# Loading q and k by tile pairs, values in quadrants, and shorter first blocks in a chunked attention and gated FFN kernel

## The chip, the core and the metric

The kernel runs on one core of a Trainium2 chip. The metric is device time in microseconds (us), as a median of several executions. A profile of one execution shows what each engine did: TensorE (PE, and PEld for its weight loads), VectorE (DVE), ScalarE (ACT), GpSimd (POOL, which here only issues DMAs and fills buffers) and SyncE (SP, which issues others).

## The reference

Four batches, eight heads, 768 positions, head dimension 64. Attention works on chunks of 32 queries: each sees 8 memory keys, 16 positions to the left of the chunk, the chunk and 8 to its right. The result, 3072 tokens of 512 features, goes through a gated feed-forward network (FFN) of 1536 hidden features.

```python
for c in range(nc):                       # 24 chunks of 32
    k_full = concat([mem_k, k[l_start:r_end]]); v_full = concat([mem_v, v[l_start:r_end]])
    scores = scale * (q_c @ k_full.T)
    a = softmax(scores)
    out[c] = a @ v_full
x = out.transpose(0, 2, 1, 3).reshape(3072, 512)
y = (relu(x @ w_gate) * (x @ w_val)) @ w_out
```

## The kernel before, in words

Work goes by tiles of 128 tokens (four chunks): 24 tiles, six to a batch, each with all eight heads. Head pairs share the 128 partitions.

For each tile, `load_qk` (L185) has POOL issue one DMA each for q and k, 1024 reads of 64 f32 (256 bytes), converted to bf16. `qk_t` (L206) transposes them on PE, four 128x128 transposes per operand, and `qk_copy` (L212) brings the result from PSUM to `qT` or `kT` on ACT or DVE. `scores` (L224) runs 32 small matmuls in tiles of 64 rows by 32 columns. Then come `row_max` (with memsets for the two edges of a batch, L245 and L247), `subtract`, three `exponent` runs on ACT, `row_sum`, `reciprocal` and `normalise`. `p_t` (L281) transposes the probabilities, `p_copy` copies them. `values` (L291) runs 16 matmuls, one for each chunk and head pair: its weights are a 128x128 block-diagonal of two heads' values in `v_bd` (56 context rows and 8 memory rows for each head, zeros off the diagonal). `x_copy` (L301) writes x transposed into `xT`.

`v_bd` has two sets of buffers. The first gets its zeros and memory rows from DVE (`pattern_spread`, L157), the second its zeros from POOL (`zero`, L114), its memory rows by 8 DMAs on SP for each batch (`mem_rows`, L138). Value rows come by POOL's DMAs (`load_v_rows`, L164), for the first batch in two halves of three tiles.

The FFN goes by blocks of tiles, `BLOCKS = [3, 3, 4, 4, 4, 4, 2]`. `first` (L311) computes for a block and a hidden group m (12 of 128 features) the gate and the value product, four matmuls each (one tile's part of the four is called a tile-group in the prediction). `relu` on ACT and `gate` on DVE follow, and `second` (L333) multiplies by `w_out`, 12 matmuls for a tile. `w_gate` and `w_val` arrive in four groups of three m each, four DMAs to a group; blocks 0 and 1 are interleaved by these groups.

The order on each engine is written out by a planner, `schedule` (L518), before launch. Each operation has its engines, an estimated cost, what it must follow, buffers that it takes and gives, and a priority; the planner simulates the engines and always starts the ready operation of lowest priority number. Attention stands before FFN, and later tiles are held to the pace of the FFN block before theirs (`pace`, L390). Loads go to POOL strictly in the order in which they are listed (L475 to L513): q and k of the first tiles, the first half of the values, the rest of q and k, the first group of weights, the second half of the values, the other weights with the zero fills, memory values, `w_out` between q and k of the second batch, and so on. What the chip then does can differ from the plan, but no engine changes its order.

PSUM buffers are 2 for transposes, probabilities and x (`aps`), 1 for scores (`sps`) and 4 for the FFN (`fps`).

Of the kernel before, what the change touches and what calls it, by code (L numbers as in the profile page):

```python
# [20 lines left out]
def kernel(  # L21
# [12 lines left out]
    nc = tc.nc  # L34
# [17 lines left out]
    BLOCKS = [3, 3, 4, 4, 4, 4, 2]  # L52
    EARLY = TPB
# [5 lines left out]
    ldpool = ctx.enter_context(tc.tile_pool(name="ldpool", bufs=18))  # L59
    kvpool = ctx.enter_context(tc.tile_pool(name="kvpool", bufs=2))  # L60
    smpool = ctx.enter_context(tc.tile_pool(name="smpool", bufs=2))
    xtpool = ctx.enter_context(tc.tile_pool(name="xtpool", bufs=2))
    gvpool = ctx.enter_context(tc.tile_pool(name="gvpool", bufs=2))
# [25 lines left out]
    vmem_f = const.tile([128, HP, 2 * D], F32, name="vmem_f")  # L89
    vmem_0 = const.tile([128, HP, 2 * D], F16, name="vmem_0")  # L90
    v_bd = [const.tile([128, HP, NCH, 2 * D], F16, name=f"v_bd_{s}") for s in range(NSET)]
# [21 lines left out]

    def zero(eng, t, hp):  # L114
        eng.memset(t[:, hp].rearrange("p c d -> p (c d)").bitcast(F32), 0.0)

# [21 lines left out]
    def mem_rows(b):  # L138
        for par in range(2):
            p = slice(64 * par + CTX, 64 * par + CTX + NMEM)  # L140
            for hp in range(HP):
                src = vmem[p, b, HP * par + hp]
                nc.sync.dma_start(
                    v_bd[b % NSET][p, hp, :, D * par:D * par + D],
                    bass.AP(tensor=src.tensor, offset=src.offset,
                            ap=[src.ap[0], [0, NCH], [1, D]]))


    def pattern_load():
        for par in range(2):  # L150
            p = 64 * par + CTX
            nc.sync.dma_start(
                vmem_f[p:p + NMEM, :, D * par:D * par + D],
# [3 lines left out]
    def pattern_spread(hp):  # L157
        src = vmem_0[:, hp]
        nc.vector.tensor_copy(
            v_bd[0][:, hp],  # L160
            bass.AP(tensor=src.tensor, offset=src.offset,
                    ap=[src.ap[0], [0, NCH], [1, 2 * D]]))

    def load_v_rows(b, par, s0, s1, c0, c1):  # L164

        dst = v_bd[b % NSET].rearrange("p h c d -> p (h c) d")
        nc.gpsimd.dma_start(  # L167
            dst[64 * par + s0:64 * par + s1, c0:c1, D * par:D * par + D],
# [16 lines left out]
    def load_qk(a, i):  # L185
        b, t = divmod(a, TPB)
        x = (q, k)[i]
        qk_b[a, i] = ldpool.tile([128, H, D], BF16, name="qk_b")
        nc.gpsimd.dma_start(  # L189
            qk_b[a, i],  # L190
            bass.AP(tensor=x.tensor, offset=x[b, 0, 128 * t, 0].offset,
                    ap=[[D, 128], [S * D, H], [1, D]]))
# [13 lines left out]
    def qk_t(a, i):  # L206
        ps = TMP["qk", a, i] = aps.tile([128, HP, 128], BF16, tag="aps", name="qk_ps")
        x = qk_b.pop((a, i))
        for hp in range(HP):
            nc.tensor.transpose(ps[:, hp, :], x[:, 2 * hp:2 * hp + 2, :].rearrange("p h d -> p (h d)"), ident_b)  # L210

    def qk_copy(a, i, eng):  # L212
        b, t = divmod(a, TPB)
        ps = TMP.pop(("qk", a, i))
        if i == 0:
            copy(eng, qT[b][:, :, 128 * t:128 * t + 128], ps)
        else:
            o = kT[b][:, :, 4 * t:4 * t + 4, :]
            copy(eng,
                 bass.AP(tensor=o.tensor, offset=o.offset,  # L220
                         ap=[o.ap[0], [NCH * KW, HP], [KW, 4], [16 + NMEM, 2], [1, 16]]),
                 ps.rearrange("p h (c x s) -> p h c x s", c=4, x=2))

    def scores(a):  # L224
        b, t = divmod(a, TPB)
        s = sps.tile([128, 2, 512], F32, name="s_ps")
# [13 lines left out]

    def row_max(a):
        t = a % TPB
        s4 = S_ps[a]
        if t == 0:
            nc.vector.memset(s4[0:CH, :, :, 0:16], NEG)  # L245
        if t == TPB - 1:
            nc.vector.memset(s4[3 * CH:4 * CH, :, :, 56:64], NEG)  # L247
# [43 lines left out]
    def values(a):  # L291
# [3 lines left out]
        for hp in range(HP):  # L295
            for g in range(4):
                r = slice(CH * g, CH * g + CH)
                nc.tensor.matmul(ps[:, hp, r], lhsT=v_bd[b % NSET][:, hp, 4 * t + g, :],  # L298
                                 rhs=x[:, hp, r], start=True, stop=True)

    def x_copy(a, eng):  # L301
# [4 lines left out]
        copy(eng, xTs[blk][:, :, 128 * j:128 * j + 128], TMP.pop(("x", a)))  # L306
# [34 lines left out]
    def store(blk, t, eng):  # L341
# [13 lines left out]
            "qk": 18, "xT": 2, "gv": 2, "gr": 3, "o": 3, "kv": 2}  # L355
# [8 lines left out]
    def psum(n):  # L364
        return {"ACT": 0.21 + 0.83e-3 * n, "DVE": 0.22 + 1.04e-3 * n}
# [16 lines left out]
    op("vm0", {"DVE": 0.5}, lambda e: nc.vector.tensor_copy(vmem_0, vmem_f), [("vml", 1.5)], prio=(-4,))  # L382
    for hp in range(HP):
        op(("spread", hp), {"DVE": 1.0}, lambda e, hp=hp: pattern_spread(hp), ["vm0"], prio=(-3 + 0.1 * hp,))
    for b in range(B):
        op(("new", b), {"DVE": 0.4}, lambda e, b=b: new_batch(b), ["kmc"], take=["kv"],
           prio=(-4.5,) if b == 0 else (1, TPB * b - 2, 0), after=[("t", TPB * b - 2, 0)] if b else [])


    def pace(a):  # L390
        blk = block_of[a]
        return [("f", blk - 1, NDC * (a - starts[blk]) // BLOCKS[blk], 0)] if blk > 1 else []

    for a in range(NT):
        b, t = divmod(a, TPB)
        last = t == TPB - 1
        for i in (1, 0):
            op(("t", a, i), {"PE": 0.24}, lambda e, a=a, i=i: qk_t(a, i), [("qk", a, i), "ib", ("new", b)],
               (1, a - i, 0), ["aps"], ["qk"], pace(max(a - i, 0)))
            op(("tc", a, i), psum(HP * 128), lambda e, a=a, i=i: qk_copy(a, i, engine[e]), [("t", a, i)],  # L400
# [243 lines left out]
```

## Time and profile before

| | us |
|---|---|
| three runs | 254.19, 255.09, 253.54 |
| median | 254.19 |
| profiled execution | 254.73 |
| its span | 252.9 |
| mean granted TensorE clock | 0.991 |
| DMA packets, of them under 512 bytes | 115051, 106320 |
| PE busy in the span | 230.6 |

The span is what the profile covers; the profiled execution has 1.8 us around it. A granted clock of 1 is full speed. A timeline line has start, length, engine, line and operation; a chain line has start, length and what the time went to. PE counts as busy while a matmul is in the array, so that its starts say more than its lengths. The clock, the packets and PE's busy time are means and sums over the whole span, whose stages differ.

### The profile page before, as it was taken

Reading aid. Unit: us, or ns where it says so; the run is one execution under the profiler, and the core shown is the slowest. Engines: PE = TensorE matmul, PEld = TensorE weight load, DVE = VectorE, ACT = ScalarE, POOL = GpSimd, SP = SyncE. Lnnn points to the kernel's source line nnn. Section 1 sums busy time; section 2 is a strip of 40 time slices with the busy share of each in tenths; the row PEclk is TensorE's granted clock in tenths of the full one; section 3 lists DMA queues with packets and bytes.
Section 4 is the critical chain, followed back from the end, with each engine's and each line's share of the span. In section 5 each row is a group of like instructions: output and inputs, shape, how many; then the busy total and the mean of one; then the engine's idle time right before and its main releaser. Section 6 shows DMA issues by size and latency. Waiting matters only on the chain.

```text
span 252.9 us, 5790 instructions
## 1 busy us (share of the span) xinstructions
PE 230.6 (91%) x2401; PEld 126.7 (50%) x2401; DVE 141.0 (56%) x259; ACT 112.5 (44%) x245; POOL 90.0 (36%) x102
## 2 busy tenths in 40 slices
PE   1546979999999799999999999999999999999993
PEld 0325555666644445555444555545555545444861
DVE  2986673577671248786167885168872274810430
ACT  3464653455443244554353553355435345432421
POOL 8999899993405575597010000000000000000000
PEclk9999998999999999999999999999999999999999
DMA  9999999999999999999991001210002200002102
GB/s 68 104 109 136 162 181 167 155 146 189 145 143 199 175 163 136 139 148 126 169 201 22 0 3 41 86 41 3 3 0 79 89 0 3 1 32 97 43 3 83
DMA packets 115051, 23.95 MB, mean 95 GB/s; under 512 B 106320, under 2 KB 111952, under 8 KB 115024
## 3 DMA queue, kind: packets, MB, share of 16 engines
q0 software_dynamic: 106400, 16.61, 94.5%
q1 hardware_dynamic: 8624, 6.97, 9.6%
q8 instruction: 19, 0.31, 0.5%
q14 instruction: 8, 0.07, 0.1%
HBM read 33.24 MB, written 6.29 MB: 156 GB/s over the span
## 4 chain that ended last, share of the span: by engine, by line
PE 77%; POOL 12%; issue 4%; DMA 4%; DVE 1%; ACT 0%; POOLq 0%
PE v_ps L317 24%; PE g_ps L317 24%; PE out_ps L338 20%; POOL qk_b L189 5%; POOL v_bd L167 5%; PE qk_ps L210 3%; PE xT_ps L298 3%; DMA w_val_sb<-in_moe_w_val_dram 2%; DMA qk_b<-in_q_dram 2%; PE s_ps L236 2%; PE pT_ps L285 1%; POOL w_gate_sb L101 1%; POOL w_val_sb L101 1%; DVE xT L77 1%; ACT o_sb L75 0%
## 5 line engine op out<-in xcount | busy, mean ns | idle before, releaser
L317 PE MATMUL g_ps<-xT,w_gate_sb 128*128 128x512 f16 (+2 forms) x336 | 77.5, 354 | 0.0
L317 PE MATMUL v_ps<-xT,w_val_sb 128*128 128x512 f16 (+2 forms) x336 | 76.8, 351 | 0.2 <-DMA w_val_sb<-in_moe_w_val_dram 0.2
L329 DVE TENSOR_TENSOR gvT<-v_ps,g_relu 128x512 f16<-128x512 f32 (+2 forms) x84 | 51.6, 614 | 42.6 <-PE v_ps L317 29.3
L323 ACT ACTIVATE g_relu<-g_ps 128x512 f16<-128x512 f32 (+2 forms) x84 | 45.0, 536 | 60.6 <-PE g_ps L317 50.5
L338 PE MATMUL out_ps<-w_out_sb,gvT 128*128 128x512 f16 x288 | 66.1, 379 | 0.0
L317 PEld LDWEIGHTS <-w_gate_sb 128*128 128x128 f16 x336 | 32.3, 99 | 27.4 <-issue 1.0
L317 PEld LDWEIGHTS <-w_val_sb 128*128 128x128 f16 x336 | 31.1, 98 | 23.0 <-issue 0.6
L338 PEld LDWEIGHTS <-gvT 128*128 128x128 f16 x288 | 26.8, 97 | 28.9
L167 POOL DMA_DIRECT2D v_bd<-in_v_dram x24 | 27.8, 1174 | 7.9 <-issue 7.8
L189 POOL DMA_DIRECT2D qk_b<-in_k_dram x24 | 22.7, 945 | 17.9 <-issue 6.9
L189 POOL DMA_DIRECT2D qk_b<-in_q_dram x24 | 22.7, 948 | 12.5 <-PE qk_ps L210 7.2
L75 ACT COPY o_sb<-out_ps 128x512 f32<-128x512 f32 x24 | 14.0, 584 | 28.9 <-PE out_ps L338 28.7
L210 PE MATMUL qk_ps<-ident_b,qk_b 128*128 128x128 bf16 x192 | 19.9, 241 | 6.3 <-DMA qk_b<-in_k_dram 3.7
L264 ACT ACTIVATE p_exp<-dif 128x256 f16<-128x256 f32 (+2 forms) x72 | 19.6, 339 | 11.2 <-DVE dif L256 11.2
L210 PEld LDWEIGHTS <-qk_b 128*128 128x128 bf16 x192 | 14.1, 106 | 12.8 <-DMA qk_b<-in_k_dram 4.9
L77 DVE CAST xT<-xT_ps 128x512 f16<-128x512 f32 x11 | 7.6, 692 | 22.4 <-PE xT_ps L298 22.3
L249 DVE TENSOR_REDUCE mx<-s_ps 128x8 f32<-128x512 f32 x24 | 16.5, 689 | 5.0 <-PE s_ps L236 4.8
L268 DVE TENSOR_REDUCE sm<-p_exp 128x8 f32<-128x512 f16 x24 | 16.3, 680 | 3.6 <-ACT p_exp L264 3.4
L75 ACT COPY pT<-pT_ps 128x512 f16<-128x512 f16 x20 | 11.7, 585 | 14.0 <-PE pT_ps L285 14.0
L279 DVE TENSOR_TENSOR p_n<-p_exp,rinv 128x512 f16<-128x512 f16 x24 | 16.5, 688 | 0.5
L256 DVE TENSOR_TENSOR dif<-s_ps,mx 128x512 f32<-128x512 f32 x24 | 16.4, 684 | 0.3
L298 PEld LDWEIGHTS <-v_bd 128*128 128x128 f16 x384 | 12.8, 98 | 6.2 <-issue 3.2
(37 smaller groups left out, 115.5 us busy)
## 6 DMA issues: line engine op xcount, KB each, us to landing
out_dram<-o_sb SPq DMA_DIRECT2D x24, 256.0 KB
v_bd<-in_v_dram POOLq DMA_DIRECT2D x5, 672.0 KB, 13.8
qk_b<-in_k_dram POOLq DMA_DIRECT2D x24, 128.0 KB, 7.5
qk_b<-in_q_dram POOLq DMA_DIRECT2D x24, 128.0 KB, 7.3
w_gate_sb<-in_moe_w_gate_dram POOLq DMA_DIRECT2D x8, 192.0 KB, 4.7
w_val_sb<-in_moe_w_val_dram POOLq DMA_DIRECT2D x8, 192.0 KB, 6.0
w_out_sb<-in_moe_w_out_dram POOLq DMA_DIRECT2D x2, 768.0 KB, 11.3
v_bd<-in_v_dram POOLq DMA_DIRECT2D x15, 84.0 KB, 5.4
```

The costliest lines, as they stand in the source:

```text
L75: nc.scalar.copy(o, i)
L167: nc.gpsimd.dma_start(dst[64 * par + s0:64 * par + s1, c0:c1, D * par:D * par + D], bass.AP(tensor=v.tensor, offset=v[b, HP * par, 0, 0].o ...
L189: nc.gpsimd.dma_start(qk_b[a, i], bass.AP(tensor=x.tensor, offset=x[b, 0, 128 * t, 0].offset, ap=[[D, 128], [S * D, H], [1, D]]))
L210: nc.tensor.transpose(ps[:, hp, :], x[:, 2 * hp:2 * hp + 2, :].rearrange("p h d -> p (h d)"), ident_b)
L249: nc.vector.reduce_max(SM[a, "mx"], s4, axis=AX.X)
L264: nc.scalar.activation(p[:, :, :, s0:s0 + k1 - k0], dif[:, :, :, k0:k1], ACT.Exp, scale=SCALE)
L279: nc.vector.tensor_tensor(out=P_n[a], in0=SM.pop((a, "p")), in1=rinv_b, op=ALU.mult)
L298: nc.tensor.matmul(ps[:, hp, r], lhsT=v_bd[b % NSET][:, hp, 4 * t + g, :], rhs=x[:, hp, r], start=True, stop=True)
L317: nc.tensor.matmul(ps, lhsT=w[:, f, 128 * m:128 * m + 128], rhs=xTs[blk][:, f, :], start=(f == 0), stop=(f == NFC - 1))
L323: nc.scalar.activation(st["r", m], st.pop((0, m)), ACT.Relu)
L329: nc.vector.tensor_tensor(out=st["gv"][:, m, :], in0=st.pop((1, m)), in1=st.pop(("r", m)), op=ALU.mult)
L338: nc.tensor.matmul(st["o", t], lhsT=st["gv"][:, m, 128 * t:128 * t + 128], rhs=w_out_sb[:, m, :], start=(m == 0), stop=(m == NDC - 1))
```

## The change

Three edits come together.

1. q and k are loaded for two tiles at once: 256 consecutive rows as 128 partitions of two adjacent rows, 1024 reads of 512 bytes. The even and odd rows are transposed apart, 16 transposes of 128x64 for a pair and operand, and the copies put them back in order with a step of two; the copies are `q_copy` for a tile and `k_copy` for even or odd rows of a pair. In the same way `x_copy` reorders.
2. The values of both heads of a pair stand in one 64-column buffer `v_sl`, one head in the upper and one in the lower 64 partitions, without zeros. Each chunk and head pair takes two 64x64 matmuls in place of one of 128x128. The zero fills go; the spread is done in two halves of the chunks.
3. The first blocks have 2, 1 and 3 tiles, in sequence and not interleaved, and `xT` and `gv` have three buffers each.

With them the list of loads changes: q and k of the first two pairs, the first half of the values, two groups of weights, q and k of the third pair, the third group of weights, the second half of the values, the fourth group, `w_out`, memory values, then q and k of the second batch. The edge memsets of the scores become an operation of their own ahead of the scores. A few copies of the first tiles are held to ACT.

```diff
-    BLOCKS = [3, 3, 4, 4, 4, 4, 2]
+    BLOCKS = [2, 1, 3, 4, 4, 4, 4, 2]
...
+    v_sl = [const.tile([128, HP, NCH, D], F16, name=f"v_sl_{s}") for s in range(NSET)]
...
-    def load_qk(a, i):
-        b, t = divmod(a, TPB)
+    def load_qk(n, i):
+        b, t = divmod(n, PPB)
         x = (q, k)[i]
-        qk_b[a, i] = ldpool.tile([128, H, D], BF16, name="qk_b")
+        qk_b[n, i] = ldpool.tile([128, H, 2 * D], BF16, name="qk_b")
         nc.gpsimd.dma_start(
-            qk_b[a, i],
-            bass.AP(tensor=x.tensor, offset=x[b, 0, 128 * t, 0].offset,
-                    ap=[[D, 128], [S * D, H], [1, D]]))
+            qk_b[n, i],
+            bass.AP(tensor=x.tensor, offset=x[b, 0, 256 * t, 0].offset,
+                    ap=[[2 * D, 128], [S * D, H], [1, 2 * D]]))
...
         for hp in range(HP):
-            nc.tensor.transpose(ps[:, hp, :], x[:, 2 * hp:2 * hp + 2, :].rearrange("p h d -> p (h d)"), ident_b)
+            for j in range(2):
+                for r in range(2):
+                    d = slice(D * r, D * r + D)
+                    nc.tensor.transpose(ps[d, hp, j, :], x[:, 2 * hp + r, D * j:D * j + D], ident_b)
...
+    def k_copy(n, j, eng):
+        b, t = divmod(n, PPB)
+        ps = TMP["qk", n, 1]
+        o = kT[b][:, :, 8 * t:8 * t + 8, j:]
+        copy(eng,
+             bass.AP(tensor=o.tensor, offset=o.offset,
+                     ap=[o.ap[0], [NCH * KW, HP], [KW, 8], [16 + NMEM, 2], [2, 8]]),
+             ps[:, :, j, :].rearrange("p h (c x s) -> p h c x s", c=8, x=2))
...
+    def edges(a):
+        s = S_ps[a] = sps.tile([128, 2, 512], F32, name="s_ps")
...
-                nc.tensor.matmul(ps[:, hp, r], lhsT=v_bd[b % NSET][:, hp, 4 * t + g, :],
-                                 rhs=x[:, hp, r], start=True, stop=True)
+                for par in range(2):
+                    d = slice(D * par, D * par + D)
+                    nc.tensor.matmul(ps[d, hp, r], lhsT=v_sl[b % NSET][d, hp, 4 * t + g, :],
+                                     rhs=x[d, hp, r], start=True, stop=True)
...
-    seq = [(blk, m) for g in range(WG) for blk in range(2) for m in range(GM * g, GM * g + GM)]
-    seq += [(0, None), (1, None)]
-    for blk in range(2, len(BLOCKS)):
+    seq = []
+    for blk in range(len(BLOCKS)):
         seq += [(blk, m) for m in range(NDC)] + [(blk, None)]
...
+    load_qk_op(0, 1)
+    load_qk_op(0, 0)
     load("ident", 0, 0, lambda: make_identity(nc, ident_h))
...
+    load_qk_op(1, 1)
+    load_qk_op(1, 0)
+    load_v_half(0, range(HP))
     load_w_op(0)
+    load_w_op(1)
+    load_qk_op(2, 1)
+    load_qk_op(2, 0)
+    load_w_op(2)
     load_v_half(1, range(HP))
...
     load_w_op(3)
-    load_zero(3)
+    for i in range(2):
+        load_wo_op(i)
```

## The prediction

> **What bounds the kernel now.** I read the busy times and slices first, then the stretches that they suggest, then the chain that ended last, then TensorE's timeline.
>
> ```profile
> PE 230.6 (91%) x2401; PEld 126.7 (50%) x2401; DVE 141.0 (56%) x259; ACT 112.5 (44%) x245; POOL 90.0 (36%) x102
> ...
> PE   1546979999999799999999999999999999999993
> ...
> POOL 8999899993405575597010000000000000000000
> ...
> DMA  9999999999999999999991001210002200002102
> ```
>
> TensorE (PE) is full from about the seventh slice to the end; before that POOL and the DMA engines are full and PE is not. So there are two stages with different limits, and the windows put numbers on them (length, then PE busy with its instruction count, PEld, DVE, ACT, POOL, clock, DMA share, GB/s):
>
> ```profile
> 20.00:38.08 18.08, 14.54 (x257) 10.02 (x258) 12.80 (x26) 10.23 (x25) 17.09 (x24) 0.96 1.70 162
> 38.08:80.00 41.92, 41.92 (x390) 24.15 (x391) 24.68 (x47) 19.57 (x45) 26.98 (x29) 0.97 1.76 161
> 80.00:87.00 7.00, 5.52 (x81) 3.23 (x80) 1.65 (x3) 1.87 (x4) 2.67 (x3) 1.00 1.65 192
> 87.00:249.08 162.08, 162.04 (x1544) 85.34 (x1542) 88.58 (x160) 70.85 (x153) 24.39 (x22) 1.00 0.73 67
> ```
>
> From 38.08 us to the last matmul at 249.07 PE loses only 1.5 us (7.00 less 5.52). The chain says what starts this stage:
>
> ```profile
> 32.59 5.35 DMA w_val_sb<-in_moe_w_val_dram
> 38.08 1.44 PE v_ps L317 x4
> 39.52 1.05 PE g_ps L317 x4
> 40.56 0.65 PE v_ps L317 x4
> ```
>
> It is the second group of FFN weights, issued by POOL until 33.2 us and landed at 38. The first two groups of matmuls then take 1.44 and 1.05 us where 0.65 is usual (the five-us window to 40 us has a granted clock of 0.68): 1.2 us of slow clock. PE's timeline prices the attention work between FFN groups (start, length, line, tile in rows*columns):
>
> ```profile
> 147.62 0.56 PE L298 MATMUL xT_ps<-pT,v_bd 128*128 128x32 f16 x16
> 148.02 0.38 PE L210 MATMUL qk_ps<-ident_b,qk_b 128*128 128x128 bf16 x4
> 148.33 0.31 PE L236 MATMUL s_ps<-kT,qT 64*32 64x64 bf16 x32
> 148.57 1.04 PE L317 MATMUL v_ps<-xT,w_val_sb 128*128 128x512 f16 x4
> 149.44 1.03 PE L317 MATMUL g_ps<-xT,w_gate_sb 128*128 128x512 f16 x4
> ```
>
> Matmul ends are modelled, so I price by starts. Values take 0.40 (25 ns each), a transpose 0.056 (chain: x8 in 0.45), the scores 0.24, and ahead of them 0.09 is lost: 148.02 + 4 x 0.056 is 148.24, and the scores start at 148.33. They are the only instructions in small tiles. Per tile of 128 tokens: q and k 0.45, scores 0.33, p transposes 0.22, values 0.40: 1.40 us. An FFN matmul takes 0.65/12, so one tile's share of one hidden group ("tile-group", 4 matmuls of 128 columns) is 0.217, and a tile's output stage 2.60 (12 matmuls).
>
> The check: before 38.08 seven groups of a three-tile block had run, 21 of 24 x 24 = 576 tile-groups. Left are 555 x 0.217 = 120.4, 24 x 2.60 = 62.4, 18 x 1.40 = 25.2, in all 208.0, against 249.07 - 38.08 = 211.0. The 3.0 between are the 1.2 of slow clock, the 1.5 of idle and 0.3. So the end is a start plus PE's remaining work: an FFN group done earlier, or an instruction made longer later on, moves the end by its own length.
>
> **Step 1, the loads and the start.** POOL's issues to the last load of the fourth weight group fall from 12 to 6 for q and k. At 0.90 each (0.78 for values, 0.63 for weights, rows of POOL's timeline): 1.26 + 6 x 0.90 + 0.6 (identity) + 17 x 0.78 + 16 x 0.63 = 30.6, and with the 4.7 us that the second group took to land, 35.3. Transfers are slower than that. The DMA view of the first 40 us shows bytes from 2 us on, some 115 GB/s while only q, k and values arrive (256-byte reads), some 190 while weights do (1.5 KB reads). Sizes are 1.38 MB of values, 3.15 of weights, 1.57 of q and k. Values 12.0 us, weights 16.6, q and k (512-byte reads, which no row shows) between 13.7 at the lower rate and 8.3 at the higher. The fourth weight group thus lands between 38.9 and 44.3; I take the middle, 41.6. The second half of the values comes 4.1 earlier, 37.5, and with 2.5 for three tiles' values and copies x(5) is there at 40.0. DVE could hold it back: q and k of tiles 4 and 5 land near 27.3 (2 + 11.0 + 6.0 + 8.3), three tiles need 3 x 2.94 of DVE (five rows of 0.20 to 0.69), the gates of the meantime 4.4, so perhaps 43; then the fourth weight group bridges with 18 tile-groups, 3.9 us. So PE is full from about 40.8 (38.1 to 43.5).
>
> By then tiles 0, 1 and 2, whose x needs only the loads that come first, have gone through three weight groups: 3 x 18 = 54 tile-groups instead of 21, at 33 x 0.217 = 7.2 us. They fit: the first weights land near 21, the third group near 31.5, and 54 x 0.217 is 11.7. The start of the full stage moves by 40.8 - 38.1 = 2.7 the wrong way. **Net -4.5** (-7.2 to -1.8). That blocks run one by one matters here alone: the same matmul columns, in narrower instructions.
>
> PE may be at full clock by then: **-0.6** of the 1.2 (0 to -1.2). The 1.5 us at 80 to 87, when values of the second batch were late and the DMA engines full, has half the q/k packets less ahead of it: **-0.7** (0 to -1.5).
>
> **Step 2, transposes.** A pair takes 16 per operand in 128x64 tiles for today's 8 of 128x128, each still 128 columns. If the two column halves run side by side, as the scores must (32 matmuls of 64 columns in 0.24 is 8 ns each), 8 rounds of 0.056 are today's 0.45. Each change of tile costs the scores' 0.09. Eighteen operations remain after the start: **+1.6** (18 x 0.09). Ends: -0.4, and 18 x (0.94 - 0.45) = +8.8 one after another.
>
> **Step 3, values.** 32 matmuls in two quadrants for 16. The nearest rows are the scores, 0.24 for as many instructions in half-row tiles, and today's values, 0.40 for 16 rounds. The quadrants have the scores' instruction count but double their weight columns, so I take the middle, 0.32, and 0.09: **+0.2** (18 x 0.01). Below, 18 x (0.33 - 0.40) = -1.3. Above: eight tiles' scores go in four rounds of 60 ns; sixteen rounds of 60 ns are 0.96, so 18 x (1.05 - 0.40) = +11.7.
>
> A page speaks against steps 2 and 3. The Trainium skill, "TensorEngine Tiling (Array Packing)", Key Properties and Restrictions, says that a change of tiling mode drains the array, which the 0.09 shows, and that column tiling rules out fast weight loads. "TensorE: Matmul & The Clock Gate", LDWEIGHTS, gives columns over 1.2 GHz: an estimate by it is 53 ns for 64 columns, 16 rounds 0.85 us, and values 9.7 us dearer over 18 tiles. No row here has a 64-column load.
>
> **Step 4, the rest, at nothing.** k copies write every second element, so DVE's 0.42 may become the 0.69 of its f32 copies; 19 such copies are 5 us of DVE's 44% idle; uncovered, each late copy would hold the scores by 0.27. The spread saves DVE half of 4.5 us, the zero fills POOL's 6.0, both off the path. The edge memsets (0.17 and 0.11) now run ahead of eight scores, which must wait for the last subtract as today, and FFN groups are queued behind them on PE: up to 8 x 0.27 = 2.2 if the written order gives no slack. Memory rows wait for both halves of memory values; on SP the output stores stand behind them, and these have three buffers. Smaller relu and gate operations add some 2 us each to ACT and DVE, which have 56% and 44% free.
>
> **Sum:** -4.5 - 0.6 - 0.7 + 1.6 + 0.2 = -4.0. The profiled execution, 254.73 with a span of 252.9, would be 250.7 with 248.9; the median, 0.54 below it, **250.2**.
>
> **Rivals.**
> 1. Narrow weights are not hidden (slower). Place: values, every tile; price: rounds of 60 ns, +11.7 in place of +0.2, so 261.7. It decides from 0.61 us for 32 matmuls (-5.8 + 1.6 + 18 x (0.70 - 0.40) = +1.2). For it: 64-column weights with only 32 columns behind which to load. Against it: full-width weights hide completely today. If instead transposes go one by one, 257.4.
> 2. The bytes count, not the reads: 512-byte reads gain nothing, the full stage starts at 43.5 or later. Then -1.8 - 0.6 + 1.8, less than a microsecond from today: 253.6 to 254. For it: DMA is full in both stages.
> 3. The start goes as well as it may and quadrants cost as the scores: -7.2 - 1.2 - 1.5 + 1.6 - 1.3 = -9.6, 244.6; say 246 with half the drains.
>
> **Chances.** Forecast 0.43, rival 1 with its dearer transposes 0.26, rival 2 0.16, rival 3 0.15. 0.5% is about what a measurement of this kernel can tell from no change. Forecast and rival 3 are faster, 0.58; rival 2 is the same, 0.16; rival 1 slower, 0.26. The range is 245 to 260: it leaves out the far end of rival 1 and the very best of rival 3. The faster cases alone would be 245 to 252.5.
>
> **What would show it.** Right: a full PE from 39 to 43 us with 54 tile-groups behind it; 16 transposes in some 0.45 and 32 value matmuls near 0.32, each with a gap of 0.09 ahead. Wrong: PE waiting for weights past 44, a values step over 0.6, or idle PE ahead of the scores of tiles 0 and 5 of a batch.

## The result and the profile after

The changed kernel takes **263.91 us** (median of four runs, 262.99 to 265.12) against 253.93 for the one before (four runs, 253.54 to 255.09): 1.0388 times as long, 95% interval 1.0333 to 1.0443, some 10 us slower. Ratios here and below compare fast runs alone while medians take all runs, so that the two can differ by some tenths of a per cent, and one run of quadrants alone, 411.62 us at a granted clock of 0.59, counts in its median only. The forecast was 250.2 us. The profiled execution took 263.80 us with a span of 262.0, 9.1 more than before.

The page of the changed kernel, lines that answer to those shown of before:

```profile
PE 241.3 (92%) x3073; PEld 136.3 (52%) x3073; DVE 137.9 (53%) x266; ACT 121.1 (46%) x260; POOL 61.9 (24%) x74
...
PE   0749986999989999999999999999999999999994
```

PE has the same share of a longer span, with 672 instructions more, and it reaches nine tenths in the fourth slice, one earlier than before. POOL has 28 us less to do. Two dips in PE's row (slice 7, 39 to 46 us, and slice 12, 72 to 79 us) are new; the dip of before at slice 14 is gone. The windows (length, then PE, PEld, DVE, ACT, POOL busy with counts, clock, DMA share, GB/s), with the same borders as before and the end where PE ends:

```profile
20.00:38.08 18.08, 17.45 (x289) 14.27 (x286) 10.54 (x24) 10.16 (x29) 12.79 (x18) 1.00 1.63 175
38.08:80.00 41.92, 37.80 (x532) 23.69 (x529) 21.63 (x48) 19.07 (x44) 18.30 (x18) 0.96 1.73 171
80.00:87.00 7.00, 7.00 (x126) 3.54 (x106) 5.34 (x10) 4.12 (x10) 4.48 (x4) 1.00 2.09 141
87.00:258.20 171.20, 170.38 (x1940) 88.15 (x1938) 88.00 (x162) 77.73 (x157) 10.28 (x9) 1.00 0.44 59
```

Ahead of 38.08 PE works 2.9 us more than before (17.45 for 14.54), and the 1.5 us at 80 to 87 are gone. In their place PE is idle for 4.1 us in the second window and 0.8 in the last, 4.9 in all. The chain of waits leads to two of the causes (start, length, what the time went to):

```profile
26.04 8.76 DMA w_val_sb<-in_moe_w_val_dram
35.08 0.77 POOL v_sl L164
35.85 1.25 POOL w_gate_sb L103 x2
...
53.50 1.82 POOL v_sl L164
55.68 21.23 DMA qk_b<-in_q_dram
...
76.96 0.64 PE qk_ps L211 x16
```

The third weight group's last load lands at 34.80, and only behind it does POOL issue the last value load and the fourth group, from 35.85 on. PE waits 1.75 us for that group's gate weights, until 42.31 (its timeline stands further below). A q load of the second batch, issued at 55.68, lands 21 us later, and PE waits 1.31 us for it. The larger cost stands in PE's timeline, in the stage where all loads have long been in:

```profile
143.28 1.03 PE L333 MATMUL g_ps<-xT,w_gate_sb 128*128 128x512 f16 x4
144.24 0.64 PE L211 MATMUL qk_ps<-ident_b,qk_b 128*64 128x128 bf16 x16
144.81 0.68 PE L312 MATMUL xT_ps<-pT,v_sl 64*64 64x32 f16 x32
145.42 1.04 PE L333 MATMUL v_ps<-xT,w_val_sb 128*128 128x512 f16 x4
```

An FFN group of four takes 0.86 us from start to start where another one follows, so that the transposes could have started near 144.15: 0.09 is lost ahead of them. From start to start, in the median of 100 to 240 us, 16 transposes take 0.57 us (8 took 0.45 before) and 32 value matmuls 0.61 (16 took 0.40). With 0.09 ahead wherever the step follows an FFN group, that is +0.21 a tile for q and k together and +0.30 for values. Eighteen tiles come after the start: 18 x 0.51 = **9.2 us**, all of the 9.1 that the span grew. So the whole of the gain expected at the start has gone as well. The timelines show it go: by 38.08 us the changed kernel had begun 52 tile-groups and the kernel before 21, but by 50 us it was 71 and 68, and the values of the changed kernel's sixth tile were still to come.

### The profile page after: what moved, and what is told of

Same layout as the page of the kernel before. It is cut to its first block, busy times and chain, and to the rows that moved or that the text cites. A ratio compares the mean times of both kernels' runs of the same rounds, so it can differ in the third digit from the quotient of the medians.

```text
span 262.0 us, 7114 instructions
## 1 busy us (share of the span) xinstructions
PE 241.3 (92%) x3073; PEld 136.3 (52%) x3073; DVE 137.9 (53%) x266; ACT 121.1 (46%) x260; POOL 61.9 (24%) x74
## 4 chain that ended last, share of the span: by engine, by line
PE 69%; DMA 16%; POOL 9%; issue 3%; ACT 1%; SPq 1%; DVE 0%; DVEq 0%; POOLq 0%
PE out_ps L354 21%; PE v_ps L333 19%; PE g_ps L333 18%; DMA qk_b<-in_q_dram 8%; POOL v_sl L164 4%; PE xT_ps L312 4%; DMA w_val_sb<-in_moe_w_val_dram 3%; PE qk_ps L211 3%; DMA w_gate_sb<-in_moe_w_gate_dram 3%; PE s_ps L244 1%; DMA vmem_f<-in_mem_v_dram 1%; PE pT_ps L297 1%; POOL w_val_sb L103 1%; POOL qk_b L187 1%; POOL w_gate_sb L103 1%
## 5 line engine op out<-in xcount | busy, mean ns | idle before, releaser
L333 PE MATMUL g_ps<-xT,w_gate_sb 128*128 128x512 f16 (+3 forms) x384 | 79.5, 331 | 2.8 <-DMA w_gate_sb<-in_moe_w_gate_dram 1.7
L333 PE MATMUL v_ps<-xT,w_val_sb 128*128 128x512 f16 (+3 forms) x384 | 79.0, 330 | 0.4 <-DMA w_val_sb<-in_moe_w_val_dram 0.2
L345 DVE TENSOR_TENSOR gvT<-v_ps,g_relu 128x512 f16<-128x512 f32 (+3 forms) x96 | 52.8, 554 | 45.4 <-PE v_ps L333 29.8
L339 ACT ACTIVATE g_relu<-g_ps 128x512 f16<-128x512 f32 (+3 forms) x96 | 46.8, 489 | 59.7 <-PE g_ps L333 53.0
L164 POOL DMA_DIRECT2D v_sl<-in_v_dram x24 | 26.8, 1122 | 46.8 <-PE s_ps L244 23.8
L76 ACT CAST xT<-xT_ps 128x512 f16<-128x512 f32 x21 | 15.2, 728 | 13.0 <-PE xT_ps L312 12.8
L211 PE MATMUL qk_ps<-ident_b,qk_b 128*64 128x128 bf16 x384 | 17.0, 237 | 3.6 <-DMA qk_b<-in_k_dram 1.8
L312 PEld LDWEIGHTS <-v_sl 64*64 64x64 f16 x768 | 15.7, 116 | 8.4 <-issue 7.6
L312 PE MATMUL xT_ps<-pT,v_sl 64*64 64x32 f16 x768 | 17.8, 186 | 1.5 <-ACT pT L76 1.3
L211 PEld LDWEIGHTS <-qk_b 128*64 128x64 bf16 x384 | 12.8, 119 | 11.9 <-issue 6.0
```

Of the source, the lines that this page charges most:

```text
L76: nc.scalar.copy(o, i)
L164: nc.gpsimd.dma_start(dst[64 * par + s0:64 * par + s1, c0:c1, :], bass.AP(tensor=v.tensor, offset=v[b, HP * par, 0, 0].offset + (CH * c0 + ...
L211: nc.tensor.transpose(ps[d, hp, j, :], x[:, 2 * hp + r, D * j:D * j + D], ident_b)
L312: nc.tensor.matmul(ps[d, hp, r], lhsT=v_sl[b % NSET][d, hp, 4 * t + g, :], rhs=x[d, hp, r], start=True, stop=True)
L333: nc.tensor.matmul(ps, lhsT=w[:, f, 128 * m:128 * m + 128], rhs=xTs[blk][:, f, :], start=(f == 0), stop=(f == NFC - 1))
L339: nc.scalar.activation(st["r", m], st.pop((0, m)), ACT.Relu)
```

## The experiments

Each run has its own runs of the kernel before beside it, whose median was 254.8 to 255.0 us; times are medians.

### What a narrow tile costs

**Wide transposes.** The changed kernel with 8 transposes of 128x128 again, each taking one head's two rows, so that q and k stand in wrong places.

```diff
-                for r in range(2):
-                    d = slice(D * r, D * r + D)
-                    nc.tensor.transpose(ps[d, hp, j, :], x[:, 2 * hp + r, D * j:D * j + D], ident_b)
+                nc.tensor.transpose(ps[:, hp, j, :], x[:, 2 * hp + j, :], ident_b)
```

> The changed kernel with 8 transposes of 128x128 per pair and operand in place of 16 of 128x64 (each takes one head's two rows, so that q and k stand in wrong places and the output is not the reference's); order of all engines unchanged. Theory A (the narrow tiles on TensorE are the loss: a pair's transposes step from start to start takes 0.66 us instead of 0.45): 18 to 24 operations of 0.21, so 3.8 to 5.0 us off, 259 to 260 us, and 0.45 in the timeline. Rival B (the start and its loads are the loss, TensorE has slack): within 1 us of 263.9.

Measured: 260.85 us, ratio 1.0261 (1.0188 to 1.0334), 3 us under the changed kernel. Eight take 0.45 with nothing lost ahead.

**Wide values.** The changed kernel with 16 value matmuls of 128x128, whose weights are two neighbouring chunks: wrong values, no zero blocks.

```diff
-                for par in range(2):
-                    d = slice(D * par, D * par + D)
-                    nc.tensor.matmul(ps[d, hp, r], lhsT=v_sl[b % NSET][d, hp, 4 * t + g, :],
-                                     rhs=x[d, hp, r], start=True, stop=True)
+                c = 4 * t + g // 2 * 2
+                nc.tensor.matmul(ps[:, hp, r], lhsT=v_sl[b % NSET][:, hp, c:c + 2, :].rearrange("p c d -> p (c d)"),
+                                 rhs=x[:, hp, r], start=True, stop=True)
```

> The changed kernel with 16 values matmuls of 128x128 per tile in place of 32 of 64x64 (weights are two neighbouring chunks, so the values are wrong); order unchanged, no zero blocks. Theory A: values 0.40 instead of 0.70 from start to start, 21 to 24 tiles, 6.3 to 7.2 us off, 256.7 to 257.6. Rival B: within 1 us of 263.9.

Measured: 259.44, ratio 1.0189 (1.0107 to 1.0270), 4.5 under the changed kernel; values are back at 0.40.

**Both**, the two edits together.

> Both of the above. Theory A: the sum, 10 to 12 us off, 252 to 254, which is the kernel before: the new loads and blocks then bring nothing. Rival B: still above 261. If the loads and blocks do bring the 5.8 us of the prediction and only the tiles were mispriced, it is below 249.

Measured: 256.79, ratio 1.0078 (1.0042 to 1.0113), 7.1 under the changed kernel, close to the sum of the two, but still 2 us above the kernel before: even with the shapes of before the new loads and blocks gain nothing. Its window at 72 to 77 us has PE waiting for the same q load, now for 3.67 us:

```profile
72.00:77.00 5.00, 1.33 (x11) 0.82 (x10) 1.42 (x4) 0.49 (x1) 1.34 (x1) 0.88 2.10 155
```

All three come out above the first theory, and this load says why. Time less PE's work at the prices above (0.66 and 0.70 for the narrow steps) is an estimate of what PE loses to waits and slow clock: from 70 to 80 us it is 1.4 us in the changed kernel, 4.5 with wide transposes, 4.0 with wide values and 5.0 with both. Most of what the wide forms save ahead of 77 us is waited away there.

**Twice.** The changed kernel with every narrow transpose and value matmul issued twice, with the same result.

```diff
-        for hp in range(HP):
+        for hp in [h for h in range(HP) for _ in range(2)]:
...
-                for par in range(2):
+                for par in (0, 1, 0, 1):
```

> The changed kernel with every 128x64 transpose and every 64x64 values matmul issued twice, same result; order unchanged. What the second copy adds is the price without the change of tile. If the rounds themselves cost (weights not hidden behind 32 columns): values step grows by 0.45 to 0.61, transposes by 0.43 to 0.57, total 280 to 287. If it is the change of tile mode that costs: values grow by 0.25 to 0.35 and the total stays below 277.

Measured: 290.35 us in its one run, at a mean granted clock of 0.959, so I go by the timeline and not by the total:

```profile
161.64 1.03 PE L333 MATMUL g_ps<-xT,w_gate_sb 128*128 128x512 f16 x4
162.60 1.08 PE L211 MATMUL qk_ps<-ident_b,qk_b 128*64 128x128 bf16 x32
163.61 1.19 PE L312 MATMUL xT_ps<-pT,v_sl 64*64 64x32 f16 x64
164.73 1.04 PE L333 MATMUL v_ps<-xT,w_val_sb 128*128 128x512 f16 x4
```

The gap ahead stays 0.09. Transposes go from 0.57 to 1.02 in the median (1.01 in these lines): 16 more cost 0.45, which is 8 rounds of 0.056. So the two column halves do run side by side, and of the 0.57 some 0.12 are spent once. Values go from 0.61 to 1.12: 32 more cost 0.51, 16 rounds of 32 ns, and 0.10 are spent once. The starts of single matmuls in the trace of the changed kernel say where: the last two transposes start 0.42 us after the first two and the next step another 0.15 later, though a round takes 0.056; the last two values start at 0.50 and the next step 0.11 later, for a round of 0.032. The remaining 0.02 go into the first round. **A visit to a narrow tile costs 0.09 on entering and 0.10 to 0.12 more, most of it on leaving.**

The scores of the kernel before have the same way out. In this window of 0.13 us, from the start of a scores step, all 32 have begun, and the next step starts at 0.24 (PE, DVE, clock, DMA share, GB/s):

```profile
105.85:105.98 0.13, 0.13 (x32) 0.00 (x0) 1.00 3.63 152
```

**Values in 64x32 tiles.** Each of the 32 as two with half the weight columns, four side by side.

```diff
...
-                    nc.tensor.matmul(ps[d, hp, r], lhsT=v_sl[b % NSET][d, hp, 4 * t + g, :],
-                                     rhs=x[d, hp, r], start=True, stop=True)
+                    for e in range(2):
...
+                        o = slice(D * par + 32 * e, D * par + 32 * e + 32)
+                        nc.tensor.matmul(ps[o, hp, r], lhsT=v_sl[b % NSET][d, hp, 4 * t + g, 32 * e:32 * e + 32],
+                                         rhs=x[d, hp, r], start=True, stop=True)
```

> The changed kernel with each of the 32 value matmuls of a tile as two in 64x32 tiles (32 columns of weights each, half the rows as before, four side by side): the same result from 64 instructions. Theory A (a round of two quadrants takes 31.6 ns because 64 columns of weights are loaded for 32 columns of data): a round of four narrower ones is shorter, the step falls from 0.61 to 0.4 to 0.5 us and the time by some 2 to 4 us. Theory B (instruction issue sets the round, some 16 ns an instruction): the step grows to 1.1, and the time by 9 us. Theory C (the columns of data set the round, and the weights do not count): the step stays at 0.6, the time within 1 us.

Measured: 266.06 in its one run, and the step as in this line and the start of the next:

```profile
108.44 0.66 PE L314 MATMUL xT_ps<-pT,v_sl 64*32 64x32 f16 x64
109.02 1.04 PE L335 MATMUL v_ps<-xT,w_val_sb 128*128 128x512 f16 x4
```

Half the weight columns and twice the instructions leave the step at 0.59 for 0.61, which looks like the third theory, though the one run is 2 us above the changed kernel. The first 0.20 us of the step say otherwise, here and in the changed kernel (PE, DVE, ACT, clock, DMA share, GB/s):

```profile
108.44:108.64 0.20, 0.20 (x32) 0.00 (x0) 0.00 (x0) 1.00 0.00 0
```

```profile
106.08:106.28 0.20, 0.20 (x12) 0.00 (x0) 0.00 (x0) 1.00 0.00 0
```

Eight rounds of four have begun, 25 ns each, where the changed kernel has begun six rounds of two, 32 ns each. The other 32 matmuls then start one by one, some 8.3 ns apart, so that four take 33 ns. So the first theory holds for the first half of the step, with 25 ns for 32 weight columns and 32 ns for 64, and the second for the other half, at half the spacing that it assumed; that they cancel in the sum is chance. The kernel before starts one full-width matmul every 25 ns. All three have 16 rounds, and no round is shorter than that.

### One part at a time

**Quadrants alone**: the kernel before with 64x64 values and no zero fills; its loads, transposes and blocks stay.

```diff
-                nc.tensor.matmul(ps[:, hp, r], lhsT=v_bd[b % NSET][:, hp, 4 * t + g, :],
-                                 rhs=x[:, hp, r], start=True, stop=True)
+                for par in range(2):
+                    d = slice(D * par, D * par + D)
+                    nc.tensor.matmul(ps[d, hp, r], lhsT=v_bd[b % NSET][d, hp, 4 * t + g, :],
+                                     rhs=x[d, hp, r], start=True, stop=True)
...
-    load_zero(0)
```

> The kernel before with values in two 64x64 quadrants without zero blocks or zero fills, alone; loads, transposes and blocks as before. Theory A (0.70 instead of 0.40 for each of the 18 values steps after the start): 5.4 us more, 259.5 to 260.5. Rival: the 6 us of POOL's zero fills that go bring the later loads forward and pay it back: below 257.

Measured: 257.49, ratio 1.0085 (1.0056 to 1.0114). That is +2.2 where 18 x 0.30 is 5.4, so the rest of the edit gave 3 us. The windows say where most of it was:

```profile
38.08:80.00 41.92, 41.92 (x424) 24.54 (x425) 24.60 (x48) 19.12 (x43) 24.88 (x27) 1.00 2.02 167
80.00:87.00 7.00, 7.00 (x150) 4.07 (x149) 1.65 (x3) 2.34 (x4) 3.09 (x2) 1.00 1.72 201
```

The 1.5 us of idle time at 80 to 87 are gone, and so are the 1.2 of slow clock behind 38.08 (a clock of 1.00 in the first window, 0.97 before).

**Blocks alone**: the kernel before with blocks of 2, 1 and 3 in sequence, three buffers for `xT` and `gv`, and 16 load buffers to make room.

```diff
-    BLOCKS = [3, 3, 4, 4, 4, 4, 2]
+    BLOCKS = [2, 1, 3, 4, 4, 4, 4, 2]
...
-    seq = [(blk, m) for g in range(WG) for blk in range(2) for m in range(GM * g, GM * g + GM)]
-    seq += [(0, None), (1, None)]
-    for blk in range(2, len(BLOCKS)):
+    seq = []
+    for blk in range(len(BLOCKS)):
```

> The kernel before with blocks of 2, 1 and 3 tiles one by one and three buffers, alone; per-tile loads in their old order, 16 load buffers instead of 18. If short first blocks bring something by themselves: 2 us or more off. If they only pay with weights that come early: within 1.3 us of the kernel before, since the second weight group still lands at 38.

Measured: 255.91, ratio 1.0038 (1.0007 to 1.0069): some 1 us, the smallest part.

**Pair loads alone**: q and k by pairs with narrow transposes and spread copies, six issues fewer; block-diagonal values, zero fills on POOL, blocks and order of the loads as before. The separate edge memsets and the copies held to ACT stay from the changed kernel.

> Part 1 of the change alone: the kernel before with q and k loaded by pairs (512-byte reads), narrow transposes and the spread copies; values stay block-diagonal with zero fills on POOL, blocks stay 3, 3, 4 and interleaved. Theory A (a change of tile costs 0.21 us at both ends, 18 times, and the faster reads give little): 254.3 + 3.8 less at most 1.5, so 256.6 to 258.5, with 16 transposes in 0.57 us and 0.09 ahead of them. Theory B (the faster reads and six issues fewer carry the start): under 255.5. Theory C (the pair loads come late, as after the change): over 259, with PE waiting for a q or k load after 70 us.

Measured: 254.48, ratio 0.9993 (0.9963 to 1.0022), the second theory. Its timeline has the 0.57 and the 0.09 of the changed kernel, 3.8 us over 18 tiles, so the loads gave 3.8 back. PE is busy throughout where it had lost 1.5 us:

```profile
80.00:87.00 7.00, 7.00 (x34) 3.13 (x32) 0.93 (x2) 1.98 (x4) 4.09 (x4) 1.00 1.86 192
```

And the reads are faster. These are the first stretches in which nearly only q and k move, 6 to 10 us, of the kernel before and of the changed one (last column GB/s):

```profile
6.00:10.00 4.00, 1.91 (x38) 1.19 (x44) 4.00 (x5) 1.59 (x4) 4.00 (x4) 1.00 1.81 115
```

```profile
6.00:10.00 4.00, 2.83 (x46) 2.35 (x48) 2.41 (x4) 1.33 (x2) 1.76 (x3) 1.00 1.77 175
```

With the DMA engines as busy (1.77 for 1.81), 512-byte reads bring 175 GB/s where 256-byte reads brought 115.

The three parts alone sum, by their ratios, to -0.2 + 2.2 + 1.0 = 3.0 us. Together they cost 10. The other 7 had to be found.

### Is it the late q load?

**The q pair earlier**: the changed kernel with the late q load listed ahead of the two large value loads of the second batch.

```diff
-    for n, i in late[:3]:
+    for n, i in late[:4]:
```

> The changed kernel with the q load of the fifth pair (tiles 8 and 9) listed ahead of the two large value loads of the second batch instead of behind them; nothing else. Theory C (besides the narrow tiles, the order of the loads loses what the start gains: in the changed kernel that q was issued at 55.7 us and landed at 77): PE's wait of 1.3 us before it goes, 262 to 263. Rival D (the DMA engines are full there and another load is late in its place): 263.5 to 264.5.

Measured: 266.09, ratio 1.0422 (1.0378 to 1.0467), no better than the changed kernel. The theory that this load's place in the list is the cause falls: the chain names the next load in the list, k of the pair after it, issued at 56.36, as the second theory had it. PE waits 3.1 us for it, and the time is above that theory's 263.5 to 264.5.

```profile
56.36 21.68 DMA qk_b<-in_k_dram
```

**The same with both shapes wide** (q, k and values wrong as above).

> The kernel with both wide forms (transposes and values as in e1 and e2, so q, k and values stand in wrong places), and that q load earlier. There the wait was 3.7 us and cooled the clock. Theory C: 3.5 to 4.5 off its 256.8, 252.3 to 253.3, that is 1 to 2 us under the kernel before. Rival D: still 256 to 257.

Measured: 258.08, ratio 1.0111 (1.0077 to 1.0145), 1.3 above the run without the move; k issued at 56.65 lands at 77.8. Whatever q or k load stands behind the two value loads lands some 21 us after the start of its issue.

### Zero fills and early weights

**Zero fills on DVE**, in the kernel before: eight memsets of half the size in place of POOL's four.

```diff
-        load(("z", hp), 0, 1.5, lambda: zero(nc.gpsimd, v_bd[1], hp))
...
+        op(("z", i), {"DVE": 0.85}, lambda e, t=t: nc.vector.memset(t, 0.0), [], (-7.5 + 0.1 * i,) if i < 4 else (3, i),
+           after=["vmem_f"] if i < 4 else [("nrm", 2)])
```

> The kernel before with one edit: the zero fills of the second batch's values (four on POOL, 1.5 us each) become eight of half the size on VectorE, four ahead of the first scores' work and four after the third tile's normalisation. Same output. Theory A (POOL's issue order holds the second batch's loads up, so the fills were not free on POOL): PE's idle of 1.5 us at 80 to 87 us goes and the second weight group is not held either; 251.5 to 252.5 against some 254.3. Theory B (the fills only fall to an engine that is as short of time at the start: VectorE's first rows come later by some 6 us of fills): 254 to 256.

Measured: 254.63, ratio 0.9989 (0.9957 to 1.0022), no difference. The profiled execution has a span of 250.9 and only 0.13 us idle from 80 to 90, but the twelve runs spread over 4 us, and taken together they are no faster. So taking the fills off POOL alone is not worth the 3 us of the quadrants run. Beside this run, that one also spares DVE the fills, half of the spread and the value loads their strided writes; which of them gave the 3 us is not settled.

**The same, and the second weight group ahead of the second half of the values.**

```diff
+    load_w_op(1)
     load_v_half(1, range(HP))
-    load_w_op(1)
```

> The kernel before with the zero fills on VectorE as in the run with that edit alone, and the second weight group listed on POOL ahead of the second half of the first batch's values. Same output. Theory A (the full stage starts when the second weight group has landed, at 38.08 us before): it lands some 6 us earlier, PE is full earlier with more FFN groups done, but the values of tiles 3 to 5 come later by as much: 1 to 2 us under the run with the fills alone, 250 to 251.5. Theory B (the bytes count: what is gained in weights is lost in the values of tiles 3 to 5, which FFN groups of the first block then can't bridge): the same as the run with the fills alone, or up to 2 us above it.

Measured: 255.25, ratio 0.9984 (0.9942 to 1.0027), no difference. PE is full from 30 to 38 us, but idle for 2.5 of the next 6: what came early in weights came late in values. That is the rival, the bytes, and it was a hint at the order of the loads.

### Where the other 7 us are

Three kernels between pair loads alone and the whole change. **The order of before**: the changed kernel with its loads listed as before, by pairs.

```diff
-    load_v_half(0, range(HP))
-    load_w_op(0)
-    load_w_op(1)
+    load_v_half(0, (0, 1))
     load_qk_op(2, 1)
+    load_v_half(0, (2, 3))
     load_qk_op(2, 0)
-    load_w_op(2)
+    load_w_op(0)
     load_v_half(1, range(HP))
...
```

> The changed kernel with one edit: its list of loads is put back in the order of before (by pairs, without the zero fills: q and k of the third pair between the two quarters of the values, the second group of weights behind the second half of the values, the output weights behind the first late pairs). Theory A (the new order of the loads loses the start: it leaves values and q/k late for tiles 3 to 5 and for the second batch): 256.5 to 259, some 6 us under the changed kernel. Theory B (blocks of 2 and 1 tiles one by one lose it, whatever the order: with one short block at a time the loads behind them are waited for): 262 to 265, as the changed kernel.

**The order and the blocks of before**: that, and blocks of 3 and 3, interleaved.

> The changed kernel with the order of loads and the blocks (3 and 3, interleaved by weight group) of before: pair loads and quadrants without zero fills alone. If the parts add up as measured alone: 254.6 - 0.2 + 2.2 = 256.6, so 255.5 to 258. If pair loads and quadrants spoil each other (for example because two narrow shapes and two gains at the start do not add: once PE is full from the first weights on, an earlier load gains nothing): 258 to 261, with PE full from 30 us on and no idle time of note behind it.

**The blocks of before** with the new order of the loads.

> The changed kernel with the blocks of before (3 and 3, interleaved by weight group) and the new order of the loads: the fourth corner. Theory A (order of the loads): 262 to 265, for tiles 3 to 5 are then needed even earlier, and their values come behind three groups of weights. Theory B (blocks): 256 to 259. If both matter, 259 to 262.

Measured, with the rows that lead to them:

| kernel | us | ratio to before (95%) |
|---|---|---|
| pair loads alone | 254.48 | 0.9993 (0.9963 to 1.0022) |
| + quadrants, no zero fills | 260.94 | 1.0242 (1.0210 to 1.0274) |
| + blocks of 2, 1, 3 | 262.03 | 1.0294 (1.0252 to 1.0337) |
| + new order of loads: the change | 263.91 | 1.0388 (1.0333 to 1.0443) |
| the change with blocks of 3, 3 | 265.35 | 1.0421 (1.0383 to 1.0459) |

Order against blocks was the wrong question: neither holds most of the loss. The order costs some 2 us, with intervals that just touch (4 with blocks of 3 and 3, where they are well apart), the blocks 1 or nothing. **The largest step is the quadrants on top of the pair loads, +6.5 us where alone they cost 2.2**, as the second theory of that run had it. Read the other way, pair loads on top of quadrants cost 3.5 (257.49 to 260.94), close to their 18 x 0.21. The windows of pair loads and quadrants together:

```profile
38.08:80.00 41.92, 41.37 (x491) 23.71 (x490) 26.98 (x51) 20.77 (x46) 18.65 (x18) 1.00 1.81 181
80.00:87.00 7.00, 7.00 (x131) 3.94 (x125) 1.69 (x3) 2.43 (x4) 4.87 (x4) 1.00 1.90 173
```

Each part alone removes PE's idle time at 80 to 87, and its slow clock behind 38.08 (the window from there has a clock of 1.00 with pair loads alone too). That gain exists once, and whichever part comes second finds PE full and pays its instructions in full. By the same estimate as above PE loses, over the whole trace, 28.2 us in the kernel before, 23.8 with quadrants alone, 22.7 with pair loads alone and 22.1 with both. So gains of 4.4 and 5.5 are 6.1 together, 3.8 less than their sum, which is most of the 4.3 by which the two runs miss it. Behind 38.08 us the kernel before loses 3.2 of its 28.2 and the other three lose nothing: that is the part that exists once.

For the order, PE's timeline of the changed kernel around 40 us shows it (in brackets what PE waited for, and how long):

```profile
39.93 0.40 PE L297 MATMUL pT_ps<-ident_h,p_n 128*128 128x128 f16 x4 [1.07 <-DVE p_n L291]
...
42.31 1.01 PE L333 MATMUL g_ps<-xT,w_gate_sb 128*128 128x256 f16 x4 [1.75 <-DMA w_gate_sb<-in_moe_w_gate_dram]
```

k and q of tiles 4 and 5 stand behind two weight groups and are transposed at 29.37 and 30.92 us (16.87 and 23.03 with the order and blocks of before). Until then DVE had waited 5.8 us for FFN groups; afterwards its rows for three tiles follow one another, and PE waits for them and for the fourth weight group. Behind these waits the clock is 0.78 from 42.31 to 50 us, some 1.7 us more.

### A version that is faster than both

The whole price of the pair loads falls on later tiles, their gain on the start. So: pair loads, narrow transposes and spread copies for the first batch only, nearly everything else as before (the separate edge memsets and the copies held to ACT stay from the changed kernel).

```diff
...
+        if a >= TPB:
+            for i in (1, 0):
+                op(("t1", a, i), {"PE": 0.24}, lambda e, a=a, i=i: qk_t1(a, i), [("qk1", a, i), "ib", ("new", b)],
+                   (1, a - i, 0), ["aps"], ["qk1"], pace(max(a - i, 0)))
...
+        elif a % 2 == 0:
```

> A version meant to be better than both: the kernel with pair loads alone, but pairs (512-byte reads, narrow transposes, spread copies) in the first batch only; the later 18 tiles are loaded and transposed as before. Same output. If the gain of pair loads is at the start and their price is 18 changes of tile of 0.21 us later on, as the theory has it: 254.3 - 0.2 - 3.8 = 250.3, so 249.5 to 252, with 8 transposes at 0.45 us and no gap ahead of them after 50 us, and PE full from 30 us. Rival (the later loads, single again, are late behind the values, as in the kernel before): PE waits at 80 to 87 us and the time is 252 to 254.5.

Measured: **251.79 us, ratio 0.9887 (0.9857 to 0.9916)**, at the upper end of the theory, and faster than both kernels. The windows and the shapes of the later tiles:

```profile
80.00:87.00 7.00, 6.87 (x92) 4.09 (x92) 2.05 (x3) 2.41 (x5) 5.36 (x6) 1.00 1.80 178
87.00:245.60 158.60, 158.60 (x1527) 83.65 (x1524) 88.47 (x160) 69.59 (x150) 21.66 (x20) 1.00 0.68 65
```

```profile
144.60 0.38 PE L230 MATMUL qk_ps<-ident_b,qk 128*128 128x128 bf16 x4
144.82 1.03 PE L364 MATMUL v_ps<-xT,w_val_sb 128*128 128x512 f16 x4
```

Four transposes take 0.22 with nothing ahead, and PE has lost 0.13 us at 80 to 87.

## Why the prediction was wrong, point by point

In the profiled span the forecast was -4.0 us and +9.1 was measured, a miss of 13.1. The values were mis-sized by 5.2 and the transposes by 2.2, and the three terms of the start and its loads, -5.8 together, came to about nothing.

- **The check.** "The end is a start plus PE's remaining work" held: the priced instructions give the change of the span, and undoing shapes gave back 3.0 and 4.5 us for 3.8 and 5.4 priced.
- **Step 2, the failed step.** "Each change of tile costs the scores' 0.09." Side by side was right: 8 rounds of 0.056. But the scores' row had shown only the entrance; the way out was inside their 0.24, of which the 32 matmuls need some 0.13, and I read all of it as work. The visit costs 0.21, so +3.8 for +1.6, inside its bounds (-0.4 to +8.8).
- **Step 3, a failed step.** "So I take the middle, 0.32." I counted instructions and columns; the runs showed that rounds count. Quadrants had 16 rounds as the kernel before, each 32 ns for 25 (0.11 of the 0.30 for a tile), and the visit came on top (0.09 and 0.10): +5.4 for +0.2. The bound above that I had written, sixteen rounds of 60 ns, asked the right question (how many rounds) with too high a price, because the scores' 0.24 holds the way out there too; their four rounds have begun within 0.13.
- **Step 1, the start, a failed step.** The forecast of the parts was fair: 512-byte reads at 175 GB/s lie near the higher rate, the fourth weight group's gate half landed at 42.2 and its last load at 44.4 (41.6 was forecast, at most 44.3), and 54 tile-groups were behind PE at 38.9 for 40.8. "So PE is full from about 40.8" failed: x(5), the last of the six tiles, for which I took 40.0 to 43, had its value matmuls at 51.15. I had seen that DVE could hold it back and then let 18 tile-groups bridge it; but probabilities and values of tiles 3 to 5 were still to be done, and PE was idle for 2.8 us from 38 to 50. So the -4.5 came to about nothing: 31 tile-groups ahead at 38, 3 at 50.
- **The clock, and 80 to 87.** The -0.6 did not come: the clock was 0.78 from 42.3 to 50, some 1.7 us lost for the 1.2 of before. The -0.7 did, in full (1.5), and was taken away by the q load at 77 (1.3).
- **Step 4.** "The zero fills POOL's 6.0, off the path": on POOL alone, yes (0.9989). k copies are dearer on DVE, 0.73 for 0.42, more than the 0.69 assumed, and so are the k and x copies on ACT, 0.73 for 0.58, which I had not counted; all that PE loses after 87 us, 0.8, is a wait for two such copies, of x on ACT. The q copies are not spread, other than the description of the change says: they leave the even and the odd rows of a chunk apart, in whole runs of 16, and the x copies put the order back. The edge memsets cost no idle time: behind 38.08 us PE waits only for p, the weights, the q load and x (1.07, 1.75, 1.31 and 0.82). The rest of step 4 was not tried by itself.
- **Rivals.** Rival 1's mechanism, dearer values, is what happened, at about half of its price: it decided from 0.61 us "for 32 matmuls", and 0.61 is what they take, before the gap. That its 261.7 comes near the measured 263.9 is luck: it has a price twice too high and a gain at the start that did not come. Rival 2, bytes and not reads, is refuted by 175 against 115. The rule of the Trainium skill, "TensorEngine Tiling (Array Packing)", Key Properties, that a change of mode drains the array, agrees with the 0.21 us lost in and out. The estimate by "TensorE: Matmul & The Clock Gate", LDWEIGHTS, of 53 ns a round was too high: 32 ns were measured with 64 weight columns, and 25 with 32 in the first half of the step in 64x32 tiles.
- **The signs.** Of those named for a wrong forecast, the values step over 0.6 came (0.61). PE's last wait for weights ended at 42.3 and not past 44, and no scores were waited for at a batch's edges.

## What to carry to other kernels

Price a visit to a smaller matmul tile as a whole, entrance and exit, and the work in it by rounds and not by instructions; where rounds do not fall, smaller tiles only cost. The starts of single matmuls in the trace of before had both, in the scores: 32 begun in 0.13 of their 0.24 us. An edit whose gain is at the start and whose price falls on every tile belongs at the start alone. And gains that cure the same wait are one gain: add the costs of edits, but not their cures.

## What the runs showed of the hardware

- A visit to a narrow tile shape costs 0.09 us ahead and 0.10 to 0.12 more, most of it behind; where two narrow steps follow each other (144.24 and 144.81 above), no gap stands between them beyond the first one's 0.12.
- A round of two value matmuls with 64 weight columns takes 32 ns. Four with 32 start every 25 ns for the first 32 matmuls of a step, and from there one matmul every 8.3 ns. A full-width one takes 25 ns.
- Copies that write every second 16-bit element cost 0.73 us on ACT and on DVE alike, against 0.58 on ACT and, for k on DVE, 0.42; q's copies, which move whole runs of 16, stay as they were. Rows of the changed kernel from 38 us on, k's spread write on ACT, q on ACT, and k's spread write on DVE:

```profile
L76 ACT COPY kT<-qk_ps 128x512 bf16<-128x512 bf16 x12 | 8.8, 730 | 1.4 <-DVE kT L78 1.2 <-PE qk_ps L211 0.2
...
L76 ACT COPY qT<-qk_ps 128x512 bf16<-128x512 bf16 x9 | 5.3, 586 | 3.8 <-PE qk_ps L211 2.1 <-DVE qT L78 1.7
...
L78 DVE COPY kT<-qk_ps 128x512 bf16<-128x512 bf16 x6 | 4.4, 730 | 7.9 <-PE qk_ps L211 4.3 <-ACT kT L76 3.6
```

- 256-byte reads brought 115 GB/s and 512-byte reads 175 in the same stretch, with the DMA engines equally busy.
- Behind two value loads of 672 KB, a q or k load of 256 KB took 21 us from issue to landing, whichever it was.
